# Half sums of two weight sets on VectorE instead of GpSimd, begun later, with VectorE in text order in two blocks

## The chip, the cores and the metric

The kernel runs on one core of a Trainium2 chip. The metric is the device time of one execution in microseconds; lower is better.

## The reference, cut to what matters

Three stages on 4608 tokens, all in fp32. First an attention in chunks of 64 tokens (batch 8, 8 heads, 576 tokens, head size 64):

```python
scores = scale * np.matmul(q_c, k_c.transpose(0, 1, 2, 4, 3))
attn = np.exp(scores - np.max(scores, axis=-1, keepdims=True))
attn = attn / (np.sum(attn, axis=-1, keepdims=True) + 1e-09)
out = np.matmul(attn, v_c)
```

Its output, laid out as x (4608 x 512), goes through a gated feed-forward (d_ff 1536):

```python
xn = x / rms * rms_g
g = xn @ w_gate
val = xn @ w_val
x2 = (g * sigmoid(g) * val) @ w_out
```

and then through a second one (d_ff 2048) with a rational function in place of the gate:

```python
h = x2 @ w_in
g = P(h) / (Q(h) + 1e-6)      # a cubic over a quadratic in |h|
return g @ w_out2
```

## The kernel before, in words

TensorE (PE) has no fp32 product of full precision here, so every operand is a pair of fp32r tensors, a high part and a low part (the value less its high part), and each product is three passes: high x high, high x low, low x high (`PASSES`). Weights arrive as 64-bit words and are turned into pairs on the chip. ScalarE (ACT) makes the high part by a cast, VectorE (DVE) the low part by a subtraction.

The tokens are nine blocks of 512. The first three, blocks 0, 1 and 2, are done plainly: a loop `plain(j)` over 12 cells (`cell`), each of which multiplies a gate column block and a value column block (24 matmuls, two *turns* of 12) and gates them: ACT takes tanh (L438), DVE two operations (L439, L455). The other six blocks go through a Strassen-Winograd scheme in three pairs (`group`, `product`, L466), which needs seven products of half size instead of eight, and in return sums of halves of its operands. The output product `w_out` does the same (L884) after a plain first block (L866). From 950 us on the last stage follows (L429 `h`, L954 `o`), which the change doesn't touch.

Everything that is no matmul of the present cell is hung on turns: `at_turn(turn, ...)` and `spread(turn, steps, gap, each, most)`, which calls the generator `steps` `each` times a turn over `most` turns; `do(turn)` runs what hangs on a turn ahead of its matmuls. Three things matter here.

- **Visits** of the attention, one tile of 128 tokens at a time (`visit`): at one turn `products` (PE `xs`, L224: attention x v of the tile before and q x k of this tile), then DVE normalizes (L262), takes the maximum (L239) and subtracts it (L241), and ACT takes exp (L248) and the square sum (L271); ACT scales (L409); some turns later `transposes` (PE `tp`, L287 and L290), which needs exp and the scaled tile, and whose results ACT (L294, L324) and DVE (L319, L326, then the denominators L253, L255, L256) take out of PSUM. `xs` and `tp` share one PSUM buffer of two banks, so each waits until the other was read. Visits come every 4 turns in block 1 and every 3 turns in block 2, with `tp` 4 and 2 turns behind `xs`.
- **`combos(g)`**, six of them, one for each of the six slabs of gate/value weights: four full adds high + low (L160, on POOL, that is GpSimd), four half-width sums on DVE (L167), then four high parts by ACT (L170) and four low parts by DVE (L172), then 14 transfers to DRAM (`wsd`), from which the Strassen blocks later load their left operands. They hang on the turns `COMBOS_AT`.
- **`left_sums(f)`**, six of them, the same for `w_out`: two adds (L732, on POOL), four half sums on DVE (L736), two high parts by ACT (L741) and two low parts by DVE (L743), at the first *items* of the output stage. An item is one step of that stage: 24 matmuls for each of the first six (plain, L866), 12 for each of the 84 after them (L884). For each item DVE subtracts the low part of `u` (L791) three items ahead into a ring of four slots, and for four of the seven products it first forms a sum (L776). Items 6 to 8 (`oa`) and 9 to 11 (`ob`) use plain pieces of `w_out`; from item 12 on the pieces `so` that `left_sums` makes are used too. `stage` (L99, L101, L107) prepares weights of the last stage, spread over this stage's items.

In which order an engine gets its instructions is decided by a list scheduler with its own costs, except for engines named by `manual_schedule`, which get them in the order of the text. Before the change that holds for the opening (all engines) and, from block 1 on, for ACT alone (`HELD`, L30). In the last stage ACT and DVE are in text order, before and after.

Of the kernel before, what the change touches and what calls it, by code (L numbers as in the profile page):

```python
# [9 lines left out]
F32 = mybir.dt.float32  # L10
# [4 lines left out]
ALU = mybir.AluOpType  # L15
# [11 lines left out]
    "120c31230a041b0d01e0f0g02001012c21c02cc3011021c310320130123013230a3212a31321432aa13424a213a43"  # L27
    "2bM3bb2b432d3bcMbdMMd4dMMde4N4deMeNgMeNMeggNNefOffNgfOggNgOggfOgOgOgO"
)
HELD = {mybir.EngineType.Activation}  # L30
UNIT_AT = (6, 10, 14)
STAGED = 6
COMBOS_AT = (22, 29, 36, 43, 50, 57)


@with_exitstack
def fused_kernel(
# [11 lines left out]
    nc = tc.nc  # L49
# [8 lines left out]
    NSB = (NB - NPL) // 2  # L58
# [95 lines left out]
    def combos(g):  # L154
        whole = buffers["w1", g][1]
        if g % 2 == 0:
            sums[0] = slab(f"sums{g}", (P, 2, U, W), F32)
        a = sums[0][:, g % 2]
        for n in range(U):
            nc.gpsimd.tensor_tensor(out=a[:, n], in0=whole[:, 0, n].bitcast(F32), in1=whole[:, 1, n].bitcast(F32), op=ALU.add)  # L160
            yield
        b = slab(f"cb{g}", (P, 2, U, W))
        b32 = b.bitcast(F32)
        h = a.rearrange("p (f m) (k c) -> p f m k c", f=2, k=2)
        a11, a12, a21, a22 = (h[:, f, :, k] for f in range(2) for k in range(2))
        for o, x, y, op in ((a22, a21, a22, ALU.add), (a21, a11, a21, ALU.subtract), (a11, a22, a11, ALU.subtract), (a12, a12, a11, ALU.subtract)):
            nc.vector.tensor_tensor(out=o, in0=x, in1=y, op=op)  # L167
            yield
        for n in range(U):
            nc.scalar.copy(b[:, 0, n], a[:, n])  # L170
            yield
            nc.vector.tensor_tensor(out=b[:, 1, n], in0=a[:, n], in1=b32[:, 0, n], op=ALU.subtract)  # L172
            yield
        hw = whole.rearrange("p two (f m) (k c) -> p two f m k c", f=2, k=2)
        hb = b.rearrange("p two (f m) (k c) -> p two f m k c", f=2, k=2)
        where = {"A11": hw[:, :, 0, :, 0], "A12": hw[:, :, 0, :, 1], "A22": hw[:, :, 1, :, 1],
                 "S1": hb[:, :, 1, :, 1], "S2": hb[:, :, 0, :, 0], "S3": hb[:, :, 1, :, 0], "S4": hb[:, :, 0, :, 1]}
        for n, name in enumerate(LEFT):
            for m in range(2):
                nc.sync.dma_start(out=wsd[:, place[2 * g + m, n]], in_=where[name][:, :, m].bitcast(F32))  # L180
        yield
# [405 lines left out]
    with ExitStack() as phase:  # L587
# [5 lines left out]
        whole = slice(0, U)  # L593
# [58 lines left out]
        def plain(j):  # L652
            for f in range(NF1):
                if j == 0 and f < NSTART:
                    continue
                do(TURN[0])
                steps = cell(j, f)
                next(steps)
                next(steps)
                TURN[0] += 1  # L660
                do(TURN[0])
                run(steps)
                TURN[0] += 1

        TURN[0] = 2 * NSTART
        plain(0)
        with tc.manual_schedule(engines=HELD):
            for j in range(1, NPL):
                plain(j)
            for n in range(NSB * STAGED):  # L670
                steps = stage(n)
                at = TURN[0] + len(ORDER) * (n // STAGED) + 4 + n % STAGED * (len(ORDER) - 12) // STAGED
                at_turn(at, next, steps)
                spread(at + 4, steps, 1, 1, 8)
# [53 lines left out]
            def left_sums(f):  # L728
                xs = [s2([P, W], f"xo{f}_{n}") for n in range(2)]
                for n, x in enumerate(xs):  # L730
                    w = wt["o", f + KH * n]
                    nc.gpsimd.tensor_tensor(out=x, in0=w[:, 0].bitcast(F32), in1=w[:, 1].bitcast(F32), op=ALU.add)  # L732
                    yield
                (a11, a21), (a12, a22) = ((x[:, :W // 2], x[:, W // 2:]) for x in xs)
                for o, x, y, op in ((a22, a21, a22, ALU.add), (a21, a11, a21, ALU.subtract), (a11, a22, a11, ALU.subtract), (a12, a12, a11, ALU.subtract)):
                    nc.vector.tensor_tensor(out=o, in0=x, in1=y, op=op)  # L736
                    yield
                for n, x in enumerate(xs):
                    k = f + KH * n
                    w = wt["so", k] = sums_o[k // U][:, :, k % U]  # L740
                    nc.scalar.copy(w[:, 0], x)  # L741
                    yield
                    nc.vector.tensor_tensor(out=w[:, 1], in0=x, in1=w[:, 0].bitcast(F32), op=ALU.subtract)  # L743
                    yield
# [7 lines left out]
            turn_o = TURN[0]  # L752
            NSTG = 2 * NF2
            for n in range(NSTG):
                steps = stage(n)
                m = n - NSB * STAGED
                if m < 0:
                    continue
                at = turn_o + m * (len(items) - 10) // (NSTG - NSB * STAGED)
                at_turn(at, next, steps)  # L760
                spread(at + 3, steps, 1, 2, 5)
            for n in range(KH):
                spread(turn_o + n, left_sums(n), 1, 5, 3)

            def sums_of(i):
                if i >= len(items) or items[i][0] is None:
# [293 lines left out]
```

## Time and profile before

| | |
|---|---|
| median of 3 timed runs | 1736.51 us (lowest 1736.25) |
| the profiled execution, its own time | 1741.44 us |
| its span, first to last instruction | 1739.7 us |
| PE busy | 1695.6 us (97%) |
| DVE busy | 1365.3 us (78%) |
| ACT busy | 1052.1 us (60%) |
| POOL busy | 320.4 us (18%) |

The profiled execution is the one whose rows are shown; 1.7 us of its time lie outside the span, and it took 4.9 us longer than the median. A busy time counts what an engine executes; what it waits for stands in other views. PEclk is the granted clock of PE, 1.00 for 2.4 GHz and 0.50 for 1.2 GHz; a stretch that lies between shows a mean of both levels.

### The profile page before, as it was taken

The page shows a single profiled execution, that of the slowest core. Times are in us where ns is not written, and L with a number is a line of the kernel's source. Part 1 is how long each engine was busy: PE and PEld are TensorE (multiplying, and loading weights), DVE is VectorE, ACT ScalarE, POOL GpSimd, SP SyncE. Part 2 cuts the span into 40 slices and gives each one's busy share as a digit, 9 for nine tenths or more (in the row PEclk, how much of TensorE's full clock was granted, in tenths as well). Part 3 has the DMA queues.
Part 4 walks back from the last instruction along what each step waited for, and adds up shares of the span by engine and source line. Part 5 has one row for each costly group of instructions (what it writes and reads, how often), then busy time and mean ns, then how long its engine had stood idle before and what let it go on. Part 6 is the DMA issues. An engine that isn't in the chain of part 4 may idle for free.

```text
span 1739.7 us, 25418 instructions
## 1 busy us (share of the span) xinstructions
PE 1695.6 (97%) x9600; PEld 1391.4 (80%) x9600; DVE 1365.3 (78%) x1951; ACT 1052.1 (60%) x1695; POOL 320.4 (18%) x294
## 2 busy tenths in 40 slices
PE   7888999999999999999999999999999999999998
PEld 6667778788878877888888888888888888888887
DVE  6867666878669678988894988787878787878786
ACT  6733244645545554555555867676767676767675
POOL 0303200000000004000001323232323232323222
PEclk9989999999999999999999999999999999999999
DMA  7874468787986998376556501010101010101000
GB/s 279 280 235 162 153 216 299 279 310 247 357 315 235 347 365 317 131 261 206 186 195 241 242 1 49 1 49 1 49 1 49 1 49 1 49 1 49 1 24 25
DMA packets 102443, 272.20 MB, mean 156 GB/s; under 512 B 10672, under 2 KB 32176, under 8 KB 97072
## 3 DMA queue, kind: packets, MB, share of 16 engines
q1 hardware_dynamic: 102176, 270.32, 43.7%
q8 instruction: 75, 1.23, 0.3%
q14 instruction: 48, 0.39, 0.1%
q10 hardware_dynamic: 144, 0.26, 0.0%
HBM read 184.55 MB, written 85.98 MB: 156 GB/s over the span
## 4 chain that ended last, share of the span: by engine, by line
PE 86%; DVE 6%; DMA 3%; ACT 2%; issue 1%; SPq 0%; POOL 0%; DVEq 0%; ACTq 0%; POOLq 0%
PE o L954 23%; PE h L429 22%; PE sa L466 8%; PE oa L884 8%; PE sb L466 6%; PE ob L884 6%; PE g L429 5%; PE v L429 5%; PE a L866 2%; PE xs L224 2%; DMA raw<-in_w_dram 1%; DMA k<-in_qkv_dram 1%; DVE c L498 1%; PE tp L290 1%; PE tp L287 1%
## 5 line engine op out<-in xcount | busy, mean ns | idle before, releaser
L954 PE MATMUL o<-w,ggring 128*128 128x512 f32 x1728 | 415.8, 390 | 0.0
L429 PE MATMUL h<-x,w 128*128 128x512 f32 x1728 | 414.8, 389 | 0.9 <-DVE T L928 0.9
L954 PEld LDWEIGHTS o<-w,ggring 128*128 128x128 f32 x1728 | 323.6, 188 | 69.5 <-DVE ob L968 2.3
L429 PEld LDWEIGHTS h<-x,w 128*128 128x128 f32 x1728 | 324.3, 188 | 68.6 <-DVE T L928 1.3
L944 POOL TENSOR_TENSOR ggring<-T,ggring 128x512 fp32r<-128x512 f32 x144 | 186.9, 1298 | 523.9 <-ACT ggring L943 281.6
L923 ACT ACTIVATE V<-h 128x512 f32<-128x512 f32 x144 | 86.0, 597 | 184.8 <-PE h L429 184.8
L926 DVE SCALAR_TENSOR_TENSOR V<-V,small,R 128x512 f32<-128x512 f32 x144 | 108.3, 752 | 84.1 <-ACT R L924 84.1
L784 ACT CAST rring<-uring 128x1024 fp32r<-128x1024 f32 x90 | 94.4, 1052 | 87.1 <-PE ob L884 33.5
L936 DVE SCALAR_TENSOR_TENSOR V<-V,R 128x512 f32<-128x512 f32 x144 | 100.0, 694 | 48.8 <-ACT R L935 48.8
L791 DVE TENSOR_TENSOR rring<-uring,rring 128x1024 fp32r<-128x1024 f32 x90 | 111.0, 1237 | 34.5 <-ACT rring L784 34.0
L937 DVE SCALAR_TENSOR_TENSOR V<-V,R 128x512 f32<-128x512 f32 x144 | 123.9, 861 | 4.9
L429 PE MATMUL g<-xT,w 128*128 128x512 f32 (+1 forms) x444 | 114.4, 407 | 2.2 <-ACT w L105 1.3
L925 ACT ACTIVATE T<-h,small 128x512 f32<-128x512 f32 x144 | 112.4, 780 | 0.0
L938 DVE SCALAR_TENSOR_TENSOR T<-T,small,V 128x512 f32<-128x512 f32 x144 | 108.2, 752 | 5.1
L466 PE MATMUL sa<-right,left 128*128 128x512 f32 x432 | 110.1, 394 | 1.7 <-DVE u L439 1.7
L928 DVE SCALAR_TENSOR_TENSOR T<-T,small,h 128x512 f32<-128x512 f32 x144 | 107.7, 748 | 5.1
L429 PE MATMUL v<-xT,w 128*128 128x512 f32 (+1 forms) x444 | 109.6, 395 | 0.0
L466 PE MATMUL sb<-right,left 128*128 128x512 f32 x432 | 108.1, 391 | 0.0
L935 ACT ACTIVATE R<-R,small 128x512 f32<-128x512 f32 x144 | 104.5, 725 | 4.7
L934 ACT ACTIVATE R<-V,small 128x512 f32<-128x512 f32 x144 | 106.2, 737 | 1.3
L429 PEld LDWEIGHTS g<-xT,w 128*128 128x128 f32 x444 | 85.3, 200 | 20.9 <-ACT w L105 1.9
L585 POOL TENSOR_TENSOR x<-x2r,x 128x512 fp32r<-128x512 f32 x36 | 48.0, 1334 | 286.7 <-ACT x L584 286.7
(157 smaller groups left out, 2714.7 us busy)
## 6 DMA issues: line engine op xcount, KB each, us to landing
left<-wsd SPq DMA_DIRECT2D x30, 2048.0 KB, 9.9
ud<-u SPq DMA_DIRECT2D x108, 256.0 KB, 3.1
uring<-ud SPq DMA_DIRECT2D x54, 512.0 KB, 4.9
raw<-in_w_dram SPq DMA_DIRECT2D x36, 512.0 KB, 5.7
w<-w2d SPq DMA_DIRECT2D x8, 2048.0 KB, 15.0
wsd<-cb SPq DMA_DIRECT2D x48, 256.0 KB, 2.7
raw<-in_w_dram SPq DMA_DIRECT2D x10, 1024.0 KB, 10.2
wsd<-w SPq DMA_DIRECT2D x36, 256.0 KB, 3.2
```

The source lines that it names most:

```text
L429: nc.tensor.matmul(out=acc[:, ts], lhsT=w[:, wh, wk], rhs=x[:, kk, xh, ts], start=kk == 0 and n == 0, stop=kk == KD - 1 and n == 2,)
L466: nc.tensor.matmul(out=acc, lhsT=lhs[:, wh, kk * P:(kk + 1) * P], rhs=rhs[:, kk, xh, :], start=start and kk == 0 and m == 0, stop=kk == 1 ...
L791: nc.vector.tensor_tensor(out=lo, in0=u_of(t, n, f), in1=hi.bitcast(F32), op=ALU.subtract)
L884: nc.tensor.matmul(out=banks[m][on], lhsT=w[:, wh], rhs=(lo if xh else hi)[:, k], start=fresh and f + k == 0 and p == 0, stop=f + k == KH ...
L925: nc.scalar.activation(out=T, in_=h, func=AF.Identity, scale=a3, bias=a2)
L926: nc.vector.scalar_tensor_tensor(out=V, in0=V, scalar=absb1, in1=R, op0=ALU.mult, op1=ALU.add)
L928: nc.vector.scalar_tensor_tensor(out=T, in0=T, scalar=a1, in1=h, op0=ALU.add, op1=ALU.mult)
L934: nc.scalar.activation(out=R, in_=V, func=AF.Ln, scale=TWO_M63, bias=lnb)
L937: nc.vector.scalar_tensor_tensor(out=V, in0=V, scalar=-2.0, in1=R, op0=ALU.add, op1=ALU.mult)
L938: nc.vector.scalar_tensor_tensor(out=T, in0=T, scalar=a0, in1=V, op0=ALU.add, op1=ALU.mult)
L944: nc.gpsimd.tensor_tensor(out=r[:, 1, :], in0=T, in1=r[:, 0, :].bitcast(F32), op=ALU.subtract)
L954: nc.tensor.matmul(out=acc2[j][m], lhsT=r[:, rh, ms], rhs=wt["q", f][:, wh, :], start=f == 0 and n == 0, stop=f == NF2 - 1 and n == 2,)
```

## The change

The adds of `combos` and of `left_sums` go from POOL to DVE. `combos` begin up to three turns later, all six now inside blocks 1 and 2. Blocks 1 and 2 (`plain(1)`, `plain(2)`) get DVE in text order beside ACT; from there on DVE is the scheduler's again. `left_sums` get four turns of three steps each instead of three of five, and start every second turn instead of every turn. The `stage` transfers of the output stage start ten items later and somewhat closer together.

```diff
--- before.py
+++ after.py
@@ -27,10 +27,9 @@
     "120c31230a041b0d01e0f0g02001012c21c02cc3011021c310320130123013230a3212a31321432aa13424a213a43"
     "2bM3bb2b432d3bcMbdMMd4dMMde4N4deMeNgMeNMeggNNefOffNgfOggNgOggfOgOgOgO"
 )
-HELD = {mybir.EngineType.Activation}
 UNIT_AT = (6, 10, 14)
 STAGED = 6
-COMBOS_AT = (22, 29, 36, 43, 50, 57)
+COMBOS_AT = (25, 31, 38, 45, 51, 58)
 
 
 @with_exitstack
@@ -157,7 +156,7 @@
             sums[0] = slab(f"sums{g}", (P, 2, U, W), F32)
         a = sums[0][:, g % 2]
         for n in range(U):
-            nc.gpsimd.tensor_tensor(out=a[:, n], in0=whole[:, 0, n].bitcast(F32), in1=whole[:, 1, n].bitcast(F32), op=ALU.add)
+            nc.vector.tensor_tensor(out=a[:, n], in0=whole[:, 0, n].bitcast(F32), in1=whole[:, 1, n].bitcast(F32), op=ALU.add)
             yield
         b = slab(f"cb{g}", (P, 2, U, W))
         b32 = b.bitcast(F32)
@@ -664,9 +663,10 @@
 
         TURN[0] = 2 * NSTART
         plain(0)
-        with tc.manual_schedule(engines=HELD):
+        with tc.manual_schedule(engines={mybir.EngineType.Activation, mybir.EngineType.DVE}):
             for j in range(1, NPL):
                 plain(j)
+        with tc.manual_schedule(engines={mybir.EngineType.Activation}):
             for n in range(NSB * STAGED):
                 steps = stage(n)
                 at = TURN[0] + len(ORDER) * (n // STAGED) + 4 + n % STAGED * (len(ORDER) - 12) // STAGED
@@ -729,7 +729,7 @@
                 xs = [s2([P, W], f"xo{f}_{n}") for n in range(2)]
                 for n, x in enumerate(xs):
                     w = wt["o", f + KH * n]
-                    nc.gpsimd.tensor_tensor(out=x, in0=w[:, 0].bitcast(F32), in1=w[:, 1].bitcast(F32), op=ALU.add)
+                    nc.vector.tensor_tensor(out=x, in0=w[:, 0].bitcast(F32), in1=w[:, 1].bitcast(F32), op=ALU.add)
                     yield
                 (a11, a21), (a12, a22) = ((x[:, :W // 2], x[:, W // 2:]) for x in xs)
                 for o, x, y, op in ((a22, a21, a22, ALU.add), (a21, a11, a21, ALU.subtract), (a11, a22, a11, ALU.subtract), (a12, a12, a11, ALU.subtract)):
@@ -756,11 +756,11 @@
                 m = n - NSB * STAGED
                 if m < 0:
                     continue
-                at = turn_o + m * (len(items) - 10) // (NSTG - NSB * STAGED)
+                at = turn_o + 10 + m * (len(items) - 20) // (NSTG - NSB * STAGED)
                 at_turn(at, next, steps)
                 spread(at + 3, steps, 1, 2, 5)
             for n in range(KH):
-                spread(turn_o + n, left_sums(n), 1, 5, 3)
+                spread(turn_o + 1 + 2 * n, left_sums(n), 1, 3, 4)
 
             def sums_of(i):
                 if i >= len(items) or items[i][0] is None:
```

What that does to the order of instructions shows in three places. In the new kernel the numbers of lines 31 to 665 are lower by one (L159 there is L160 here); from 669 on they are the same.

DVE in block 1, before, from the subtraction for tile 11 (`p11`) to the readout of the next transposes (`xf10`, read from `tp10_11`); `sums` and `cb` are the half sums and their parts, `u1_5` is cell 5 of block 1:

```order
L241 TENSOR_TENSOR p11_1587<-xs10_11_1547,mx11_1588 128x2x4x64
L253 TENSOR_REDUCE den11_1686<-p11_1587 128x8
L172 TENSOR_TENSOR cb1_1493<-sums0_1173,cb1_1493 128x512 x2
L439 SCALAR_TENSOR_TENSOR u1_5_1630<-u1_5_1630,g1_5_1616 128x512
L255 TENSOR_SCALAR den11_1686<-den11_1686 128x8
L167 TENSOR_TENSOR sums2_1652<-sums2_1652 128x2x256
L172 TENSOR_TENSOR cb1_1493<-sums0_1173,cb1_1493 128x512
L455 TENSOR_TENSOR u1_5_1630<-u1_5_1630,v1_5_1617 128x512
L172 TENSOR_TENSOR cb1_1493<-sums0_1173,cb1_1493 128x512
L256 RECIPROCAL den11_1686<-den11_1686 128x8
L167 TENSOR_TENSOR sums2_1652<-sums2_1652 128x2x256 x3
L439 SCALAR_TENSOR_TENSOR u1_6_1669<-u1_6_1669,g1_6_1655 128x512
```

Behind its last row stands L319 `xf10`. The same stretch of DVE's order after the change:

```order
L240 TENSOR_TENSOR p11_1568<-xs10_11_1528,mx11_1569 128x2x4x64
L166 TENSOR_TENSOR sums0_1292<-sums0_1292 128x2x256 x2
L454 TENSOR_TENSOR u1_4_1507<-u1_4_1507,v1_4_1494 128x512
L166 TENSOR_TENSOR sums0_1292<-sums0_1292 128x2x256 x2
L438 SCALAR_TENSOR_TENSOR u1_5_1626<-u1_5_1626,g1_5_1612 128x512
L171 TENSOR_TENSOR cb1_1593<-sums0_1292,cb1_1593 128x512
L454 TENSOR_TENSOR u1_5_1626<-u1_5_1626,v1_5_1613 128x512
L171 TENSOR_TENSOR cb1_1593<-sums0_1292,cb1_1593 128x512
L438 SCALAR_TENSOR_TENSOR u1_6_1662<-u1_6_1662,g1_6_1648 128x512
L318 TENSOR_TENSOR xf10_1563<-tp10_11_1665,small_64 128x512
```

Where eight operations of `combos` stood in a bunch, two now stand between one operation of the cells and the next, and the denominators stand behind the transposes.

DVE in block 2, before, from the subtraction for tile 14 to the readout of `tp13_14`:

```order
L241 TENSOR_TENSOR p14_2188<-xs13_14_2148,mx14_2189 128x2x4x64
L253 TENSOR_REDUCE den14_2244<-p14_2188 128x8
L439 SCALAR_TENSOR_TENSOR u2_2_2210<-u2_2_2210,g2_2_2196 128x512
L255 TENSOR_SCALAR den14_2244<-den14_2244 128x8
L256 RECIPROCAL den14_2244<-den14_2244 128x8
L455 TENSOR_TENSOR u2_2_2210<-u2_2_2210,v2_2_2197 128x512
L319 TENSOR_TENSOR rawx0_2103<-tp13_14_2230,small_64 128x4x128
```

The same stretch of DVE's order after the change (L159 are the adds that were POOL's):

```order
L240 TENSOR_TENSOR p14_2170<-xs13_14_2130,mx14_2171 128x2x4x64
L171 TENSOR_TENSOR cb3_1962<-sums2_1746,cb3_1962 128x512
L159 TENSOR_TENSOR sums4_2113<-w4_768 128x512 x2
L438 SCALAR_TENSOR_TENSOR u2_2_2193<-u2_2_2193,g2_2_2179 128x512
L166 TENSOR_TENSOR sums4_2113<-sums4_2113 128x2x256 x2
L454 TENSOR_TENSOR u2_2_2193<-u2_2_2193,v2_2_2180 128x512
L318 TENSOR_TENSOR rawx0_2096<-tp13_14_2228,small_64 128x4x128
```

And ACT's order there, after the change (L247 is exp, L169 the cast whose result the L171 above needs, L437 tanh, L408 the scaling that `tp13_14` needs):

```order
L270 ACTIVATE xf13_2165,ssq13_2166<-xa13_2163 128x512
L247 ACTIVATE p14_2170<-p14_2170 128x512
L169 CAST cb3_1962<-sums2_1746 128x512
L437 ACTIVATE u2_2_2193<-g2_2_2179 128x512
L408 ACTIVATE xa13_2163<-xa13_2163,ssq13_2166 128x512
L293 COPY pT14_2237<-tp13_14_2228 128x512
```

Five full-width operations of `combos` now stand between the subtraction and the readout, where none stood, and the first of them needs a cast that stands behind exp.

DVE in the output stage, before, from the last eviction of the plain block (L803, at the end of item 5) on; the L791 below are those of items 9 to 12:

```order
L803 TENSOR_SCALAR x2_0_3_7069<-a0_3_6828 128x512
L736 TENSOR_TENSOR xo5_1_7027<-xo5_1_7027,xo5_0_7026 128x256
L743 TENSOR_TENSOR so1_6790<-xo5_0_7026,so1_6790 128x512
L776 TENSOR_TENSOR uring0_6784<-uring1_6785,uring0_6784 128x1024
L743 TENSOR_TENSOR so2_6791<-xo5_1_7027,so2_6791 128x512
L791 TENSOR_TENSOR rring0_6787<-uring2_6786,rring0_6787 128x2x512
L791 TENSOR_TENSOR rring1_6788<-uring2_6786,rring1_6788 128x2x512
L776 TENSOR_TENSOR uring2_6786<-uring2_6786,uring0_6784 128x1024
L791 TENSOR_TENSOR rring1_6788<-uring2_6786,rring1_6788 128x2x512
L99 TENSOR_SCALAR raw2_19_7019<-raw2_19_7019 128x512
L776 TENSOR_TENSOR uring2_6786<-uring2_6786,uring0_6784 128x1024
L101 ISA raw2_19_7019<-raw2_19_7019,t_7115 128x512x2
```

The same place after the change; the L791 below are those of items 9 to 11:

```order
L803 TENSOR_SCALAR x2_0_3_7020<-a0_3_6822 128x512
L732 TENSOR_TENSOR xo3_0_7049<-w0_6082 128x512
L791 TENSOR_TENSOR rring0_6790<-uring2_6789,rring0_6790 128x2x512
L743 TENSOR_TENSOR so0_6792<-xo2_0_6979,so0_6792 128x512
L732 TENSOR_TENSOR xo3_1_7050<-w2_6533 128x512
L743 TENSOR_TENSOR so2_6794<-xo2_1_6980,so2_6794 128x512
L736 TENSOR_TENSOR xo3_1_7050<-xo3_0_7049,xo3_1_7050 128x256
L791 TENSOR_TENSOR rring1_6791<-uring2_6789,rring1_6791 128x2x512
L736 TENSOR_TENSOR xo3_0_7049<-xo3_0_7049 128x256
L776 TENSOR_TENSOR uring2_6789<-uring2_6789,uring0_6787 128x1024
L736 TENSOR_TENSOR xo3_0_7049<-xo3_1_7050,xo3_0_7049 128x256
L791 TENSOR_TENSOR rring1_6791<-uring2_6789,rring1_6791 128x2x512
```

Before, `left_sums` was all but done here and a `stage` came in between; now `left_sums(3)`, `(4)` and `(5)` stand behind L803, and the `stage` has moved away. From L803 to the L791 of item 14, that one included, the order before has 6 L791, 5 L776, 1 L736, 2 L743 and the 3 operations of one `stage`; the order after has 6 L791, 4 L776, 9 L736, 5 L743 and 6 L732. From there to the L791 of item 15 it is 2 L818, 1 L776 and the L791 before, and the same with 1 L743 and 2 L736 more after. From there to the L791 of item 16 it is 1 L776 and the L791 before, and the same with 1 L736 and 1 L743 more after.

## Rows read from the trace of the kernel before

**Rows 1.** The page, parts 1 and 4: busy times, and the chain that ended last.

```profile
PE 1695.6 (97%) x9600; PEld 1391.4 (80%) x9600; DVE 1365.3 (78%) x1951; ACT 1052.1 (60%) x1695; POOL 320.4 (18%) x294
...
PE 86%; DVE 6%; DMA 3%; ACT 2%; issue 1%; SPq 0%; POOL 0%; DVEq 0%; ACTq 0%; POOLq 0%
```

**Rows 2.** Stretches of the span; the first row names the columns, DMA comes last.

```profile
core 0: us, PE busy (x) PEld busy (x) DVE busy (x) ACT busy (x) POOL busy (x), PEclk, DMA share, GB/s
73.00:100.00 27.00, 21.49 (x161) 16.85 (x163) 23.72 (x33) 13.69 (x20) 14.62 (x11) 0.87 0.78 266
168.00:180.00 12.00, 6.36 (x78) 5.05 (x78) 11.10 (x16) 1.71 (x4) 4.72 (x5) 0.72 0.38 132
215.00:225.00 10.00, 8.13 (x58) 5.98 (x60) 7.86 (x15) 4.58 (x9) 0.89 (x2) 0.83 0.44 136
225.00:300.00 75.00, 75.00 (x816) 61.74 (x806) 51.21 (x92) 32.50 (x62) 5.17 (x14) 1.00 0.77 271
676.00:685.30 9.30, 5.12 (x20) 3.25 (x19) 9.20 (x11) 5.00 (x6) 9.30 (x7) 0.97 0.74 233
685.30:693.00 7.70, 7.68 (x21) 6.07 (x22) 7.60 (x11) 1.24 (x2) 1.09 (x1) 0.59 1.02 402
720.00:950.00 230.00, 230.00 (x1017) 190.44 (x1016) 182.52 (x191) 128.42 (x159) 6.66 (x4) 1.00 0.61 205
```

**Rows 3.** Waits of PE, whole span: us in total, times, longest us.

```profile
PE xs L224 <- DVE xf L319: 7.5, 3, 5.6
PE tp L287 <- ACT p L248: 7.2, 5, 4.0
...
PE a L866 <- DVE rring L791: 3.2, 1, 3.2
```

**Rows 4.** DVE by form, 159.7 to 172.2 us: busy us, mean ns, idle before.

```profile
L172 DVE TENSOR_TENSOR cb<-sums,cb 128x512 fp32r<-128x512 f32 x4 | 6.1, 1554 | 0.0
L167 DVE TENSOR_TENSOR sums<-sums 128x512 f32<-128x512 f32 x2 | 3.4, 1699 | 0.0
...
L455 DVE TENSOR_TENSOR u<-u,v 128x512 f32<-128x512 f32 x1 | 0.7, 675 | 0.0
```

**Rows 5.** DVE by form, 180 to 199 us, same columns.

```profile
L172 DVE TENSOR_TENSOR cb<-sums,cb 128x512 fp32r<-128x512 f32 x4 | 2.7, 687 | 0.4 <-ACT cb L170 0.4
...
L167 DVE TENSOR_TENSOR sums<-sums 128x512 f32<-128x512 f32 x1 | 0.7, 681 | 0.0
```

**Rows 6.** The tile sums: ns shortest/median/longest, first and last start.

```profile
L160 POOL TENSOR_TENSOR sums<-w x24: 1267/1517/2295, 73.1 to 208.3; 128x512 f32<-128x512 f32 x24
```

**Rows 7.** Timeline in block 2: start, length, engine, line, what ended the wait.

```profile
234.94 0.69 PE L224 MATMUL xs<-v,pT 64*64 64x64 f32 x32
...
238.32 0.63 ACT L248 ACTIVATE p<-p 128x512 f32<-128x512 f32 x1 [0.60 <-DVE p L241]
...
238.85 0.60 ACT L170 CAST cb<-sums 128x512 fp32r<-128x512 f32 x1
...
244.68 0.69 DVE L326 TENSOR_TENSOR right<-rawx,right 128x512 fp32r<-128x512 f32 x1 [0.69 <-ACT right L324]
...
245.31 0.56 PEld L224 LDWEIGHTS xs<-v,pT 64*64 64x64 f32 x32 [0.35 <-issue]
```

**Rows 8.** Timeline of the output stage: its entry, and items 14 and 15.

```profile
674.12 2.88 DVE L486 TENSOR_TENSOR u<-u,c 128x512 f32<-128x512 f32 x2
...
683.57 5.04 DVE L791 TENSOR_TENSOR rring<-uring,rring 128x1024 fp32r<-128x1024 f32 x3
...
735.34 1.21 DVE L791 TENSOR_TENSOR rring<-uring,rring 128x1024 fp32r<-128x1024 f32 x1
...
736.48 1.28 DVE L818 SCALAR_TENSOR_TENSOR c11o<-ob,c11o 128x512 f32<-128x512 f32 x2
...
738.81 1.21 DVE L791 TENSOR_TENSOR rring<-uring,rring 128x1024 fp32r<-128x1024 f32 x1
...
744.58 6.74 PE L884 MATMUL ob<-rring,so 128*128 128x512 f32 x29
```

## The prediction, made before the changed kernel ran

> **What bounds the kernel now.** I read the page first: its busy times and the chain that ended last. PE is busy 97% of the span and carries 86% of that chain [rows 1], so only time in which PE stands idle, or runs at a lower clock, can be won; it is lost in few places. Second, the table of stretches [rows 2]: length less PE's busy time is idle, busy time times (1 less PEclk) is about what the clock takes. In 225 to 300 us, which is block 2 of the plain loop, and from 720 to 950 us, PE has no idle time and the full clock: nothing can be won there, only lost. Four stretches remain, each of them one in which POOL adds or the bunch of DVE work behind them run:
>
> - A, 73 to 100 us, block 0: 5.5 us idle, 21.5 x 0.13 = 2.8 us by the clock.
> - B, 168 to 180 and 215 to 225 us, block 1: 5.6 + 1.9 us idle, 1.8 + 1.4 by the clock, 10.7 together.
> - C, 676 to 693 us, the entry of the output stage: 4.2 us idle, 3.1 by the clock.
>
> That is 8.3 + 10.7 + 7.3 = 26.3 us in all. Third, PE's waits [rows 3]: the longest ones are for DVE's readout of transposes (5.6 us once), for exp, which follows a DVE subtraction (4.0 us once), and for DVE's first low part of the output stage (3.2 us). So DVE is late there. Fourth, why: DVE by form. While POOL adds, a low part of `combos` takes 1554 ns and a half sum 1699 ns; an operation on data from PSUM keeps its 675 ns [rows 4]. Without POOL the same two forms take 687 and 681 ns [rows 5]. So a POOL add, 1.27 to 2.3 us long [rows 6], slows just those DVE operations that read two SBUF tensors, by some 0.9 to 1.0 us each.
>
> **The change part by part.**
>
> *The adds of `combos` leave POOL.* 24 adds of 1.5 us disappear there, 24 of the form and size of a low part, 0.69 us, appear on DVE. Instructions that follow one another without a wait start 0.07 us less than their length apart (an L791 of 1.21 us starts at 735.34, the next at 736.48 [rows 8]), so 24 x 0.61 = 15 us of DVE time, spread over blocks 1 and 2. Where POOL stood in the way:
>
> A. Eight adds and eight half sums leave block 0 altogether, and nothing takes their place. In the order of DVE nothing of the visits there changes but that. I expect 3.2 of the 5.5 us idle back: the 4.0 us wait for exp shrinks to about 1.3, because some 2.7 us of stretched DVE operations (at about 1 us each) lie ahead of that subtraction, and 0.5 us comes back at the readout of the transposes before. The wait at 75 us, some 1 us, is ACT's own queue. The clock fell after the 4 us; with 1.3 us left I take half of its 2.8 us back. A: 3.2 + 1.4 = 4.6 us. Bounds: 2 us (only part of the idle time) and 8.3 us.
>
> B. The two stalls of block 1 go, with their clock: 10.7 us. What takes their place is DVE in text order. A visit in block 2 has 10.37 us (234.94 to 245.31 [rows 7]). DVE then issues six full operations of the visit and two small ones (3.6 + 0.4 us), three of the cells (1.8) and, 12 operations of `combos` spread over 6.5 turns, 5.5 of those (3.3): 9.1 us, which would fit. But two waits stand in the text: L326 for its cast (0.69 us [rows 7]), and a low part L172 for a cast that on ACT stands behind exp: exp starts 0.60 us after the subtraction, takes 0.63, and the cast 0.60 [rows 7], so DVE stands some 1.3 us there. 11.1 us against 10.4: DVE falls 0.7 us further behind in each visit in which a low part follows the subtraction. What is queued behind that L172 is the rest of `combos`, the gating of the cells and the next L319, for which PE's next `xs` waits; the scaling and exp for `tp` come late in the same way. The order has five such visits in block 2 and two, with 4 turns and some 2.7 us more, in block 1. I take 3.0 us in block 2 and 0.5 in block 1. B: 10.7 - 3.5 = 7.2 us. Bounds: 10.7 (the two turns between `xs` and `tp` swallow all of it) and -4 (each of twelve visits loses the whole 1.25 us of exp and cast).
>
> *The adds of `left_sums` leave POOL.* C. At the entry two L486 took 2.88 us and three L791 5.04 us [rows 8], against 2 x 0.68 and 3 x 1.21: 1.5 and 1.4 us too much, and a few more beside them. Against that two adds (1.2 us) now stand on DVE ahead of the first L791. I put the start of PE 2.7 us earlier of the 4.2, and half of the clock's 3.1 back: 4.2 us. But the six last adds, and with them most of `left_sums(3)` to `(5)`, now stand behind L803, which waits for the end of item 5. From there to the low part of item 14 DVE has, against before, 6 adds, 3 L743 and 8 half-width sums more, one L776 and the three operations of a `stage` less: 3.6 + 1.8 + 8 x 0.36 - 1.14 - 1.55 = 5.6 us. Before, that low part was ready at 736.5 us, and item 14 began at 744.58 less the 2.7 us of 12 matmuls, 741.9 [rows 8]: 5.3 us in hand, now -0.3. For item 15 come 0.6 + 2 x 0.36 = 1.3 us more, and 4.6 us were in hand (738.81 + 1.21 to 744.58 [rows 8]): -2.3. For item 16 another 1.0 us, with about 5 in hand: -3. After that the products without a sum let DVE catch up. So PE loses about 3.0 us there, which it didn't before, and such a wait in two or three pieces close together should cost some clock as well; for this I take 1.5 us, half of what the entry lost. C: 4.2 - 3.0 - 1.5 = -0.3 us. Bounds: 6 (PE's start comes back whole and the scheduler's other order of matmuls at item 14 hides the rest) and -8.
>
> At the entry of the output stage DVE is busy 9.2 of 9.3 and 7.6 of 7.7 us [rows 2]. The Trainium skill, "Perfetto Trace Analysis", section "Optimizing Scalar/DVE Operations", says that where DVE is saturated, moving some of its work to ScalarE or even GpSimd may make sense, and adds that between DVE and GpSimd it might not help, because they share a read port of SBUF. By the first half `left_sums` belongs on POOL: C would lose its 4.5 us and also its 4.2 us, and the sum would be 11.8 us. By the second half `combos` belongs on DVE, and rows 4 and 5 agree.
>
> *The rest.* The DMA issues of `combos` move with their sums, three turns later at most in the first and one in the last; the transfers are read no sooner than item loads in the Strassen blocks, so I cost this at nothing. `stage` begins ten items later with an interval of 5.0 instead of 5.7 items; it is hidden in a stage in which DVE is busy 182.5 of 230 us [rows 2].
>
> *Sum.* 4.6 + 7.2 - 0.3 = 11.5 us. The profiled execution would take 1741.44 - 11.5 = 1729.9, and the timed runs 1736.5 - 11.5 = 1725.
>
> **The rivals.**
>
> 1. *All of it comes back, DVE's text order costs nothing.* For it: 9.1 us of DVE work fit into a visit, and PE's two turns between `xs` and `tp` are a cushion. Against it: the waits for casts. 8.3 + 10.7 + 6 = 25 us: 1711.
> 2. *The gain is given back.* Idle time shrinks, but pieces of 1 to 2 us remain in the same places and draw the clock down as before, and the output stage loses its 4.5 us in full: A 2, B 3, C -5: 1736. For it: after stalls of 1.9 us in all the clock fell in 215 to 225 us too [rows 2].
> 3. *Slower: DVE in text order sets the pace of blocks 1 and 2.* Place: the low part L172 behind exp in ACT's queue. Price: 1.25 us in each of 12 visits, 15 us, and 3 us of clock, against the 10.7 us that B had to win: -7; with C at -6 and A at 2 that is 11 us more: 1748. It decides from the point where DVE's queue, at the next `tp`, is more than PE's cushion late, some 3 us.
> 4. *The change doesn't do what it says*, because POOL's adds were not what made DVE late, but the visits themselves. Against it: the two lengths of one form in rows 4 and 5. It ends near 1736, with rival 2.
>
> **How the numbers follow.** The forecast, 1718 to 1731, has 0.5; rival 1 0.12; rivals 2 and 4 0.25; rival 3 0.13. A range of 1714 to 1738 leaves out rival 3 and the better half of rival 1, some 0.2. About 2%, 35 us, is what a measurement of this kernel tells from no change, and it is more than the 26.3 us that can be won at all: faster 0.01. Slower by 35 us needs three times rival 3: 0.02. Within: 0.97.
>
> **What would show it.** Right: no POOL row longer than 1 us before 950 us apart from those of L585; low parts of 0.69 us throughout; no idle time of PE in 168 to 180 us, and PE at the end of block 1 some 10 us sooner than before; waits of 0.3 to 0.8 us for exp, the scaling or L319 in block 2; and a wait of PE for L791 in items 14 to 16, some 60 us into the output stage. Wrong: block 2 longer than before by more than 5 us; no wait in items 14 to 16; the clock still down for 7 us in block 0 or at the entry of the output stage.

## The result, and the profile after

Median of four runs 1722.95 us (1719.71 to 1724.88), beside 1736.82 us for the kernel before: ratio 0.9919, 95% interval 0.9897 to 0.9942. One of the four runs of the kernel before was a slow one of 2415.91 us; the ratio goes by the other three, 1736.25 to 1737.12 us. The medians differ by 13.9 us, inside the range and 2 us below the forecast of 1725. The profiled execution took 1724.88 us, its span is 1723.1 us, 16.6 less than before. PE executes the same 9600 matmuls in 8.5 us less, which is the clock, and its idle time fell from 44.1 to 36.0 us. Part 1 of the page after:

```profile
PE 1687.1 (98%) x9600; PEld 1383.8 (80%) x9600; DVE 1368.8 (79%) x1987; ACT 1050.5 (61%) x1695; POOL 264.6 (15%) x258
```

Stretches of the changed kernel, columns as in [rows 2]; everything after 73 us lies up to 16.6 us earlier than before, so the entry of the output stage is now in 660 to 676 us:

```profile
73.00:100.00 27.00, 25.01 (x234) 20.09 (x233) 21.92 (x36) 16.72 (x26) 2.45 (x5) 1.00 0.90 302
130.00:168.00 38.00, 37.65 (x354) 30.92 (x354) 30.74 (x53) 14.77 (x29) 2.21 (x6) 1.00 0.47 160
168.00:180.00 12.00, 12.00 (x59) 10.03 (x58) 10.31 (x19) 4.26 (x8) 0.00 (x0) 1.00 0.37 131
180.00:215.00 35.00, 34.56 (x277) 28.27 (x276) 25.77 (x43) 12.75 (x24) 1.48 (x4) 1.00 0.66 219
215.00:225.00 10.00, 9.82 (x103) 7.67 (x101) 8.93 (x16) 2.61 (x6) 0.61 (x2) 1.00 0.51 159
225.00:300.00 75.00, 73.17 (x695) 58.83 (x696) 59.06 (x106) 36.31 (x72) 4.55 (x13) 1.00 0.81 286
660.00:676.00 16.00, 14.83 (x64) 11.63 (x63) 15.56 (x24) 6.06 (x7) 0.00 (x0) 1.00 0.97 339
676.00:685.30 9.30, 9.30 (x43) 7.70 (x42) 7.40 (x13) 3.15 (x4) 0.00 (x0) 1.00 1.00 385
720.00:950.00 230.00, 226.76 (x999) 186.97 (x999) 186.13 (x206) 136.19 (x174) 9.28 (x6) 1.00 0.68 234
```

All these stretches now have the full clock, where [rows 2] had 0.87, 0.72, 0.83 and 0.59. One stretch between them has not: 118 to 124 us, at 0.73, behind a wait of 1.4 us for L318. The kernel before has the same wait and the same loss 6 us later, in 118 to 130 us, which the prediction's list leaves out. The long waits are gone, small ones are new. PE's waits, to be held against [rows 3]:

```profile
PE tp L286 <- ACT p L247: 4.0, 6, 1.0
PE sa L465 <- DVE u L438: 2.9, 1, 2.9
PE oa L884 <- ACT so L741: 2.4, 1, 2.4
PE xs L223 <- DVE xf L318: 1.8, 2, 1.4
PE a L866 <- DVE rring L791: 0.9, 1, 0.9
```

The tiles of `combos` (ns shortest/median/longest, first and last start; the last row is what ended DVE's idle time ahead of them, us and times). All adds are DVE's, all operations have one length, but DVE stands 8.8 us before low parts:

```profile
L159 DVE TENSOR_TENSOR sums<-w x24: 681/685/689, 125.7 to 238.8; 128x512 f32<-128x512 f32 x24
L171 DVE TENSOR_TENSOR cb<-sums,cb x24: 640/686/696, 142.3 to 258.6; 128x512 fp32r<-128x512 f32 x24
...
  ACT cb L169: 8.8, 8
```

One of these eight places, in block 2 (timeline): the low part stands behind exp and a cast, as forecast.

```profile
224.81 0.63 ACT L247 ACTIVATE p<-p 128x512 f32<-128x512 f32 x1 [0.60 <-DVE p L240]
225.35 0.60 ACT L169 CAST cb<-sums 128x512 fp32r<-128x512 f32 x1
225.50 0.66 PE L286 MATMUL tp<-ident,p 128*128 128x128 f32 x4 [0.68 <-ACT p L247]
...
225.99 0.69 DVE L171 TENSOR_TENSOR cb<-sums,cb 128x512 fp32r<-128x512 f32 x1 [1.20 <-ACT cb L169]
```

And item 14 of the output stage. PE waits there (the other 0.85 us idle since 720 us belong to the last stage), but for the high part L741 of `left_sums(5)`, which stands behind an L736 that comes late on DVE, not for a low part L791:

```profile
724.27 1.21 DVE L776 TENSOR_TENSOR uring<-uring,uring 128x1024 f32<-128x1024 f32 x1
725.40 0.41 DVE L736 TENSOR_TENSOR xo<-xo,xo 128x256 f32<-128x256 f32 x1
...
725.85 0.62 ACT L741 CAST so<-xo 128x512 fp32r<-128x512 f32 x1 [2.82 <-DVE xo L736]
726.52 1.20 PE L884 MATMUL oa<-rring,so 128*128 128x512 f32 x4 [2.39 <-ACT so L741]
```

### The profile page after: what moved, and what is told of

It is laid out like the page before. It is cut to its first block, busy times and chain, and to the rows that moved or that the text cites. A ratio compares the mean times of both kernels' runs of the same rounds, so it can differ in the third digit from the quotient of the medians.

```text
span 1723.1 us, 25397 instructions
## 1 busy us (share of the span) xinstructions
PE 1687.1 (98%) x9600; PEld 1383.8 (80%) x9600; DVE 1368.8 (79%) x1987; ACT 1050.5 (61%) x1695; POOL 264.6 (15%) x258
## 4 chain that ended last, share of the span: by engine, by line
PE 80%; DVE 9%; issue 4%; DMA 3%; ACT 3%; POOL 1%; SPq 0%; POOLq 0%; DVEq 0%; ACTq 0%
PE o L954 21%; PE h L428 21%; PE sa L465 8%; PE oa L884 7%; PE sb L465 6%; PE ob L884 5%; PE g L428 4%; PE v L428 3%; PE a L866 2%; PE xs L223 1%; DMA k<-in_qkv_dram 1%; DVE c L497 1%; PE tp L286 1%; POOL ggring L944 1%; DVE u L438 1%
## 5 line engine op out<-in xcount | busy, mean ns | idle before, releaser
L791 DVE TENSOR_TENSOR rring<-uring,rring 128x1024 fp32r<-128x1024 f32 x90 | 109.2, 1221 | 27.1 <-ACT rring L784 26.3
```

The lines of the kernel that those rows point to most:

```text
L791: nc.vector.tensor_tensor(out=lo, in0=u_of(t, n, f), in1=hi.bitcast(F32), op=ALU.subtract)
```

## The experiments

Twelve kernels in three groups, each group with the kernel before on the same chip (medians 1738.97, 1738.72 and 1738.24 us), so groups are compared by ratio; 0.001 is 1.74 us. All edits but one are to the changed kernel.

**1. The `combos` part alone.** `left_sums` and `stage` as before.

```diff
-                    nc.vector.tensor_tensor(out=x, in0=w[:, 0]...
+                    nc.gpsimd.tensor_tensor(out=x, in0=w[:, 0]...
-                at = turn_o + 10 + m * (len(items) - 20) // ...
+                at = turn_o + m * (len(items) - 10) // ...
-                spread(turn_o + 1 + 2 * n, left_sums(n), 1, 3, 4)
+                spread(turn_o + n, left_sums(n), 1, 5, 3)
```

> The changed kernel with its second part undone: the adds of left_sums on POOL again, in the old turns, and the stage turns as before. It has the combos part and DVE's text order alone. Theory (the second part is worth some 3.7 us net: 6.1 won at the entry of the output stage, 2.4 lost at item 14): the wait for DVE's L791 at the entry is back at 3 to 4 us with the clock at half after it, the wait of 2.4 us for ACT's L741 at item 14 is gone, time 1725 to 1729. Rival (the entry was late only because everything before it was late, not because of POOL's adds): entry wait stays near 1 us, time 1720 to 1722, lower than the changed kernel because the loss at item 14 goes.

1724.63 us, ratio 0.9919 (0.9905 to 0.9933). The entry wait is back and the one at item 14 is gone. Timeline at the entry:

```profile
657.29 12.95 POOL L732 TENSOR_TENSOR xo<-w 128x512 f32<-128x512 f32 x8 [0.69 <-DVE u L438]
657.67 3.16 DVE L485 TENSOR_TENSOR u<-u,c 128x512 f32<-128x512 f32 x2
...
667.41 5.05 DVE L791 TENSOR_TENSOR rring<-uring,rring 128x1024 fp32r<-128x1024 f32 x3
...
669.15 11.23 PE L866 MATMUL a<-rring,w 128*128 128x512 f32 x41 [3.17 <-DVE rring L791]
```

Eight adds in a row on POOL: two L485 take 3.16 us, three L791 5.05 us, as in [rows 8]. So POOL makes the entry late, not what lies before it. The time was a shade under what I expected: beside the changed kernel's own ratio (experiment 5) it is no difference. The wait is as long as in the kernel before, but less of the clock went with it (stretch, columns as in [rows 2]): 11.52 x 0.11 = 1.3 us, where that kernel lost 3.1.

```profile
660.00:676.00 16.00, 11.52 (x41) 8.37 (x41) 15.90 (x20) 6.55 (x9) 10.24 (x7) 0.89 0.85 302
```

**2. The `left_sums` part alone**, on the kernel before: the two lower parts of the diff above forwards, nothing else.

```diff
-                    nc.gpsimd.tensor_tensor(out=x, in0=w[:, 0]...
+                    nc.vector.tensor_tensor(out=x, in0=w[:, 0]...
-                at = turn_o + m * (len(items) - 10) // ...
+                at = turn_o + 10 + m * (len(items) - 20) // ...
-                spread(turn_o + n, left_sums(n), 1, 5, 3)
+                spread(turn_o + 1 + 2 * n, left_sums(n), 1, 3, 4)
```

> The kernel before with the second part alone: adds of left_sums on DVE, the new turns of left_sums and of stage; combos and DVE's order in blocks 1 and 2 as before. Theory: the stalls in blocks 0 and 1 stay (4.0 us for exp, 5.6 us for the readout, clock under 0.9 there), the entry of the output stage starts as in the changed kernel, one wait of 2.4 us at item 14; 3 to 4 us faster than before, 1733. Rival (the parts only help together): within 1 us of before.

1736.65 us, ratio 0.9986 (0.9976 to 0.9995): 2.4 us. The waits in blocks 0 and 1 stand (5.6 and 4.0 us), the entry wait is 0.9, the wait for L741 2.4 us. As the theory has it, somewhat less than its 3 to 4 us.

**3. DVE left to the scheduler** in blocks 1 and 2, adds on DVE.

```diff
-        with tc.manual_schedule(engines={mybir.EngineType.Activation, mybir.EngineType.DVE}):
+        with tc.manual_schedule(engines={mybir.EngineType.Activation}):
             for j in range(1, NPL):
```

> The changed kernel, but DVE in blocks 1 and 2 is the list scheduler's again (ACT alone in text order). In the scheduler's order the first eight adds stand in block 0 again, on DVE now. Theory (the adds on POOL made the stalls, the text order costs the 2.8 us of small stalls in block 2): waits in block 2 below 1 us in all; but eight adds of 0.69 us and as many half sums are back in block 0, on a DVE that is busy there 0.87 of the time, so a wait of PE of 1 to 3 us between 73 and 100 us; time 1720 to 1727. Rival (the text order is what helps, because it spreads the operations of combos): bunches of adds ahead of a readout, waits of 3 to 5 us in block 0 or 1 with the clock down, time 1730 to 1738.

1719.96 us, ratio 0.9891 (0.9876 to 0.9906). With the adds on DVE the text order, then, is not what helped; it costs some 2 to 5 us (0.0028 here, beside the changed kernel of another group; 2.2 us between experiments 6 and 8). Idle time of PE is 1.0 us in 73 to 100 us, though adds stand in block 0, and 1.2 in 225 to 300 us, 0.5 of which the kernel before has too.

**4. The adds of `combos` on POOL again**, later turns and text order kept.

```diff
-            nc.vector.tensor_tensor(out=a[:, n], in0=whole[:, 0, n]...
+            nc.gpsimd.tensor_tensor(out=a[:, n], in0=whole[:, 0, n]...
```

> The changed kernel, but the 24 adds of combos on POOL again, at the later turns and with DVE in text order. Theory (a POOL add slows the DVE operations that read two SBUF tensors by 0.9 to 1.0 us each): block 0 stays clean since no add stands in it, the low parts and half sums of blocks 1 and 2 that meet a POOL add take 1.3 to 1.7 us, and since DVE's queue in blocks 1 and 2 holds back what PE waits for, PE loses 4 to 10 us there against the changed kernel: 1727 to 1733. Rival (the spread by text order and the later start were what helped, not the engine): DVE has 15 us less to do and the time is 1718 to 1722.

1735.86 us, ratio 0.9981 (0.9972 to 0.999): 11 us of the gain are lost, more than I expected, and one premise fell. The later turns don't keep the adds out of block 0: POOL's order is the scheduler's, which pulls eight of them there. Timeline:

```profile
74.27 13.35 POOL L159 TENSOR_TENSOR sums<-w 128x512 f32<-128x512 f32 x8
...
93.05 0.65 PE L286 MATMUL tp<-ident,p 128*128 128x128 f32 x4 [4.04 <-ACT p L247]
...
214.71 11.30 POOL L159 TENSOR_TENSOR sums<-w 128x512 f32<-128x512 f32 x8 [6.83 <-PE v L428]
...
219.02 0.63 ACT L270 ACTIVATE xf<-xa 128x512 f32<-128x512 f32 x1 [4.60 <-DVE xa L261]
...
226.10 0.51 POOL L272 TENSOR_SCALAR ssq<-ssq 128x1 f32<-128x1 f32 x1
...
228.06 1.11 PE L289 MATMUL tp<-ident,xa 128*128 128x128 f32 x4 [6.22 <-ACT xa L408]
```

The 4.0 us wait of block 0 is there as before. The 6.2 us are another mechanism, which I had not thought of: the scaling L408 needs a tiny operation of POOL (L272) on the square sum, ready at 219.7 us, and it stands in POOL's queue behind eight adds until 226.10.

**5. The changed kernel once more**, beside the next three, with no edit.

> The changed kernel itself once more, to stand on the same chip beside the three runs that follow. Both theories: the ratio of its first measurement, 0.990 to 0.994.

1723.12 us, ratio 0.9919 (0.9904 to 0.9933).

**6. `left_sums` at its old turns**, adds on DVE.

```diff
-                spread(turn_o + 1 + 2 * n, left_sums(n), 1, 3, 4)
+                spread(turn_o + n, left_sums(n), 1, 5, 3)
```

> The changed kernel with one line undone: left_sums again at one item after the other, five steps a turn (the adds stay on DVE, the stage turns stay new). In this order all of left_sums stands on DVE ahead of L803, inside the plain items of 24 matmuls. Theory (the 2.4 us wait of item 14 for ACT's L741 is the lateness of left_sums(5), which the new, slower spread causes): the wait goes, the entry wait stays at 0.9 us, 1.5 to 3.5 us faster than the changed kernel. Rival (DVE has no room in the plain items, so the low parts L791 come late there instead): new waits of PE for L791 between 670 and 700 us, 1 to 4 us, and no gain.

1719.07 us, ratio 0.9893 (0.9878 to 0.9909): 4 us faster than experiment 5. PE is busy 229.15 of 230 us from 720 us on (226.76 above), and has no wait between the entry and 760 us. DVE has room for all of `left_sums` in the plain items of 24 matmuls; the wait of item 14 is the price of the slower spread.

**7. Adds on POOL, and POOL in text order too.** DVE's and ACT's orders are those of experiment 4; only POOL's differs.

```diff
-            nc.vector.tensor_tensor(out=a[:, n], in0=whole[:, 0, n]...
+            nc.gpsimd.tensor_tensor(out=a[:, n], in0=whole[:, 0, n]...
-        with tc.manual_schedule(engines={mybir.EngineType.Activation, mybir.EngineType.DVE}):
+        with tc.manual_schedule(engines={mybir.EngineType.Activation, mybir.EngineType.DVE, mybir.EngineType.Pool}):
```

> As the run with the adds of combos on POOL, but POOL in text order in blocks 1 and 2 as well, so that the adds start where the text has them and not in block 0; DVE's and ACT's orders are those of that run. Theory (it is POOL's adds beside DVE that cost, wherever they stand): block 0 as clean as in the changed kernel (25 us busy of 27 from 73 us, no clock loss), but low parts and half sums of 1.3 to 1.7 us in blocks 1 and 2 and 4 to 9 us of PE's waits and clock more there than in the changed kernel; 1726 to 1733. Rival (it is the bunch in block 0 that cost, and the engine does not matter): within 2 us of the changed kernel.

1721.29 us, ratio 0.9906 (0.9892 to 0.9921). The rival holds: 13 us (0.0075) from one engine's order, and no difference from the changed kernel that can be told. Eight adds in a row are there, at a harmless place (timeline, and the stretch, columns as in [rows 2]):

```profile
166.01 11.85 POOL L159 TENSOR_TENSOR sums<-w 128x512 f32<-128x512 f32 x8
...
171.99 3.45 DVE L166 TENSOR_TENSOR sums<-sums 128x512 f32<-128x512 f32 x2 [1.04 <-POOL sums L159]
```

```profile
168.00:180.00 12.00, 12.00 (x58) 10.02 (x57) 10.06 (x13) 2.30 (x4) 9.86 (x7) 1.00 0.37 131
```

Two half sums take 3.45 us beside the adds instead of 1.36, and PE waits for nothing there. That the text order, with few operations of `combos` between a subtraction and the next readout, leaves the room for it is how I read this; experiment 9 tries it.

**8. Experiments 3 and 6 together.**

```diff
-        with tc.manual_schedule(engines={mybir.EngineType.Activation, mybir.EngineType.DVE}):
+        with tc.manual_schedule(engines={mybir.EngineType.Activation}):
...
-                spread(turn_o + 1 + 2 * n, left_sums(n), 1, 3, 4)
+                spread(turn_o + n, left_sums(n), 1, 5, 3)
```

> The changed kernel with two edits that each did or should do well: DVE in blocks 1 and 2 left to the list scheduler, and left_sums at their old turns (adds on DVE). Theory (the two are independent): 1716 to 1719, ratio to before 0.986 to 0.989, and no wait for L741. Rival (what is won ahead of the output stage is lost again to transfers or the clock): not below the run with the scheduler's order alone, 0.989 or more.

1716.86 us (1715.48 to 1718.26), ratio 0.9878 (0.9863 to 0.9894): the fastest of all, 1.2% under the kernel before and 0.4% under the changed one. There is no wait for L741, as the theory has it.

**9. As 8, but adds on POOL, with POOL in text order.**

```diff
-            nc.vector.tensor_tensor(out=a[:, n], in0=whole[:, 0, n]...
+            nc.gpsimd.tensor_tensor(out=a[:, n], in0=whole[:, 0, n]...
-        with tc.manual_schedule(engines={mybir.EngineType.Activation}):
+        with tc.manual_schedule(engines={mybir.EngineType.Activation, mybir.EngineType.Pool}):
```

> As the run with the scheduler's DVE and left_sums at their old turns, but the adds of combos on POOL, with POOL in text order in blocks 1 and 2 and DVE the scheduler's. Theory, formed after the run with POOL's adds late (the engine of the adds does not matter; what costs is eight POOL adds in a row in block 0, where DVE has no slack): block 0 clean, 1714 to 1720, ratio 0.986 to 0.990. Rival (with the adds on POOL it is DVE's text order that keeps block 1 clean; without it the bunch of low parts and half sums behind POOL's adds is back): waits of 3 to 6 us for DVE's L318 between 160 and 180 us and the clock below 0.9 there, 1722 to 1728.

1724.03 us, ratio 0.9917 (0.9904 to 0.9931): block 0 is clean, but with the scheduler's DVE the engine does matter, 0.0039 or 7 us. The rival holds in its time and its mechanism. Its place was wrong: from 160 to 180 us PE has neither idle time nor a lower clock, the waits stand elsewhere, and they are 2 us and not 3 to 6. Timeline in block 1:

```profile
139.93 4.71 POOL L159 TENSOR_TENSOR sums<-w 128x512 f32<-128x512 f32 x3
...
140.27 3.21 DVE L171 TENSOR_TENSOR cb<-sums,cb 128x512 fp32r<-128x512 f32 x2
...
147.19 2.09 DVE L166 TENSOR_TENSOR sums<-sums 128x512 f32<-128x512 f32 x3
...
149.80 0.68 DVE L318 TENSOR_TENSOR xf<-tp,small 128x512 f32<-128x512 f32 x1
...
150.54 0.89 PE L223 MATMUL xs<-v,pT 64*64 64x64 f32 x32 [2.02 <-DVE xf L318]
```

Two low parts take 3.21 us beside the adds, a bunch of `combos` stands ahead of the readout, and PE waits 2.0 us; 1.15 and 1.97 us more follow at 220.18 and 242.97 us.

**10. Casts one step ahead** of the subtractions that need them, in the changed kernel.

```diff
-        for n in range(U):
-            nc.scalar.copy(b[:, 0, n], a[:, n])
-            yield
-            nc.vector.tensor_tensor(out=b[:, 1, n], in0=a[:, n], ...)
-            yield
+        for n in range(U + 1):
+            if n < U:
+                nc.scalar.copy(b[:, 0, n], a[:, n])
+                yield
+            if n > 0:
+                nc.vector.tensor_tensor(out=b[:, 1, n - 1], in0=a[:, n - 1], ...)
+                yield
```

> The changed kernel with combos' casts one step ahead of the subtractions that need them, so that a low part L171 in DVE's text order never stands behind a cast of the same turn. Theory (what the text order costs is the low part that waits for a cast behind exp; DVE stands 8.8 us there in eight waits): that idle time falls below 2 us, the waits of PE for p and xa in blocks 1 and 2 from some 4 us to below 2, 2 to 3 us faster than the changed kernel, ratio 0.990 to 0.991. Rival (it is the mere number of operations between the subtraction and the next readout): DVE's idle time for casts falls, PE's waits do not, ratio 0.9915 to 0.993.

1725.46 us, ratio 0.9925 (0.9912 to 0.9937). DVE's idle time for casts falls from 8.8 to 1.2 us, and PE's in 225 to 280 us from 0.88 (experiment 5) to 0.02. But the gain is lost at once. Timeline at the first visit behind block 2 (two lines were added, so L240 is the maximum, L242 the subtraction, L249 exp), and the stretches, columns as in [rows 2]:

```profile
286.75 0.69 DVE L240 TENSOR_REDUCE mx<-xs 128x8 f32<-128x512 f32 x1
...
287.34 0.69 DVE L355 TENSOR_TENSOR rawx<-rawx 128x512 f32<-128x512 f32 x1
...
287.94 0.69 DVE L242 TENSOR_TENSOR p<-xs,mx 128x512 f32<-128x512 f32 x1
...
289.35 0.66 PE L288 MATMUL tp<-ident,p 128*128 128x128 f32 x4 [2.28 <-ACT p L249]
```

```profile
225.00:280.00 55.00, 54.98 (x550) 44.61 (x551) 40.26 (x74) 22.27 (x44) 3.69 (x10) 1.00 0.84 298
280.00:300.00 20.00, 17.42 (x135) 13.67 (x134) 16.16 (x29) 10.65 (x21) 0.95 (x2) 0.91 0.61 197
```

There DVE is the scheduler's again, and its order now has an L355 between maximum and subtraction: a wait of 2.3 us, and the clock at 0.91 behind it. The time is the rival's, the cause is not: the low parts behind exp do make PE wait in block 2, but to take that away gained nothing.

**11. Casts ahead, and `left_sums` at its old turns**: the diffs of 10 and 6 together.

```diff
-                spread(turn_o + 1 + 2 * n, left_sums(n), 1, 3, 4)
+                spread(turn_o + n, left_sums(n), 1, 5, 3)
```

> The changed kernel with the casts one step ahead and left_sums at their old turns on DVE. If both edits count by themselves: 3 to 4 us for left_sums and 2 to 3 for the casts, 1716 to 1719, ratio 0.987 to 0.989. If the casts do nothing: as left_sums alone, 0.9893.

1722.33 us, ratio 0.9908 (0.9895 to 0.9922): no better than 6 alone (0.9893; the intervals overlap). The 2.3 us wait of experiment 10 is here too.

**12. As 11, with the adds on POOL and POOL in text order**: the diff of 7 on top.

```diff
-            nc.vector.tensor_tensor(out=a[:, n], in0=whole[:, 0, n]...
+            nc.gpsimd.tensor_tensor(out=a[:, n], in0=whole[:, 0, n]...
-        with tc.manual_schedule(engines={mybir.EngineType.Activation, mybir.EngineType.DVE}):
+        with tc.manual_schedule(engines={mybir.EngineType.Activation, mybir.EngineType.DVE, mybir.EngineType.Pool}):
```

> The run before this one with the adds of combos on POOL, POOL in text order in blocks 1 and 2. Theory (engine of no account when the adds stand late; 15 us less on DVE): 1714 to 1718, ratio 0.986 to 0.988. Rival (the low parts that meet an add, 1.1 to 1.7 us long, take back what the casts and the lighter DVE give): 0.989 or more.

1722.28 us, ratio 0.9906 (0.9892 to 0.9919): the same as 11, so the rival's number. A second pair, after 5 and 7, in which with DVE in text order the engine of late adds makes no difference that can be told.

Two parts of the change were not undone by themselves: the later turns of `combos`, and the later `stage` turns. What they are worth alone is not shown.

## Why the prediction was right, point by point

The time was right; the sum of 11.5 us was made of one term near its size (B) and two that were too small. For the profiled execution the forecast of 1729.9 us missed by 5.0; that the median came within 2 us is in part luck, as said below the sum.

- **A.** 6.3 us instead of 4.6. Idle time 5.5 to 2.0, 3.5 beside the 3.2 forecast; the wait for exp in block 0 fell from 4.0 to 1.0 us. The mis-sized term is the clock: I took half of 2.8, all came back. The mechanism is shown by experiments 4 and 7, where POOL's order alone brings it back and takes it away.
- **B.** 8.4 us, forecast 7.2. The stalls went whole, 10.7. (The one in 215 to 225 us lies in block 2: its 24 turns of 12 matmuls begin at 207.5 us in the kernel before. The sum stays.) Idle time from 130 us on is 2.8 us (0.35, 0.44, 0.18 and 1.83 us by stretch), but 0.5 of it is the first wait of PE for L354, in the Strassen blocks, which the kernel before has too, only behind 300 us. So the new waits of the text order cost 2.3 us against 3.5. The rows are waits of PE, after in 200 to 300 us and before in 300 to 660 us:

```profile
PE sa L465 <- ACT rightt L354: 0.5, 1, 0.5
PE sa L466 <- ACT rightt L355: 0.5, 1, 0.5
```

  But the reason given, that POOL's adds make DVE late, is half of it: in experiment 7 the adds are on POOL and the stalls stay away, in 3 DVE is the scheduler's and they stay away too. It takes both, slowed operations and a bunch of them ahead of a readout; the change removed both.
- **C.** 3.7 us, forecast -0.3; the worst term. The entry gave back 6.1 of 7.3 (1.2 us idle left, full clock), I had 4.2, and again took half the clock. The loss was 2.4 us where I had 4.5: the step that counted DVE operations ahead of L791 found the right item and the wrong operand, and no clock was lost. The 3.7 us are what the two profiles show; as a part by itself it is worth less: the kernel without it (experiment 1) is as fast, the kernel with it alone (2) gains 2.4 us.
- **Not in the sum:** a wait in the Strassen blocks, 1.7 us before and 2.9 after, -1.2. In the other runs it is 0.8 to 3.0 us, 2.3 in experiment 5 with the same kernel, so nothing shows that the change lengthened it. ACT, in text order, stands at an L92 for a transfer, and a tanh that PE needs is queued behind it:

```profile
606.46 1.72 ACT L92 ACTIVATE raw<-raw 128x1024 f32<-128x1024 f32 x2 [8.88 <-DMA raw<-in_wo_dram]
...
612.24 0.59 ACT L437 ACTIVATE u<-sa 128x512 f32<-128x512 f32 x1
...
614.04 1.67 PE L465 MATMUL sa<-right,left 128*128 128x512 f32 x6 [2.89 <-DVE u L438]
```

6.3 + 8.4 + 3.7 - 1.2 = 17.2 us, where the spans differ by 16.6. The clock's share in it is 9.1 us, reckoned from the means of PEclk, and PE's busy time fell by 8.5. The medians differ by 13.9, since the profiled execution of before stood 4.6 us above its median and that of after 1.9.

Rival 1 (25 us) fell at the text order's stalls and item 14, rival 2 because the clock stayed up and C gained. Rival 3 fell: the new waits in block 2 are 0.3 to 0.7 us, 2.0 us in all, not 1.25 us a visit; experiment 3 does show its sign, text order costs. Rival 4 fell, but for B the engine was indeed not all. Of the signs named, the wait for L791 did not come, and two tiny POOL operations (L273) took 1.1 us; the others came, the end of block 1 some 14 us sooner instead of 10.

The Trainium skill, "Perfetto Trace Analysis", section "Optimizing Scalar/DVE Operations", says that moving operations between DVE and GpSimd might not help. The runs say that their place in time weighs more: POOL's adds cost 13 us or nothing by where its queue has them (4 against 7), and the engine decides 7 us only where DVE's order is the scheduler's (8 against 9).

## What to carry to other kernels

Before work is moved from a slower engine to a loaded one, ask first whether it only runs at the wrong time: an engine whose order a scheduler sets may start work well ahead of the turn that the text hangs it on, as POOL did with eight adds in experiment 4, and a bunch of it can slow a neighbour and block short operations in its own queue. Size a stall together with the clock that fell behind it in the trace (half of it was too little in A and at the entry), and undo the parts of a change one by one: here one part of it (text order) and one half of another (the slower spread) took away 7 us of what the rest had won.

## What was not expected of the hardware

- The prediction has POOL's adds slow just the DVE operations that read two SBUF tensors. One with a single SBUF input is slow beside them too: in experiment 4, from 74 to 88 us, L254 on 128x8 took 0.76 us (0.17 without adds); in the kernel before, in the window of [rows 4], the same operation took 0.66. L98, like L254 a tensor-scalar operation, kept its 0.69. L100, an add of two SBUF tensors of integers, took 2.02 us in the mean (1.22 without adds). The Trainium skill, "SBUF — State Buffer", section "Who interferes with whom", has contention for two SBUF inputs, and for one input only in some modes of such operations. No run here tells the modes apart.
- The clock does not answer alike to like waits. The changed kernel and experiments 3 and 8 have a wait of 1.40 us for L318 at the same place, ending at 116.71, 115.75 and 116.91 us; in 118 to 124 us the granted clock was 0.73 in the first and 1.00 in the other two. Why is not settled. The stretches of the changed kernel, of experiment 3, and of the kernel before, 6 us later, columns as in [rows 2]:

```profile
118.00:124.00 6.00, 6.00 (x61) 4.59 (x58) 1.81 (x6) 0.60 (x1) 0.00 (x0) 0.73 0.24 87
118.00:124.00 6.00, 6.00 (x56) 4.74 (x55) 2.96 (x5) 1.95 (x4) 0.74 (x2) 1.00 0.09 33
124.00:130.00 6.00, 6.00 (x60) 4.46 (x60) 0.80 (x2) 0.60 (x1) 0.00 (x0) 0.72 0.32 118
```
